# All engines in emission order: attention as a table of stages with lags, side work in slots of the weight stream, and a reordered tail

## The chip, the cores and the metric

The kernel runs on one core of one Trainium2 chip. The metric is the device time of one execution in microseconds (us). Runs of one kernel scatter by about 1% here (before: 522.9 to 529.3). Rounds ran on different chips, so kernels of different rounds are compared by their ratios to the kernel before. Each kernel has one profile, so a start or a wait is one reading. "First acc" is the start of the first weight matmul. PE is the matmul engine (PEld its weight loads), DVE the vector engine, ACT the scalar engine, POOL the GpSimd engine, SP the engine that issues the DMAs.

## The reference, cut to what matters

```python
# q, k, v: (8 batches, 8 heads, 576, 64), float32
scores = q @ k.T / 8, causal, window 128, ALiBi bias      # attention
x = softmax(scores) @ v   ->  (8, 576, 512)
X = rfft(x, axis=1)                                       # first 64 modes only
Y[m] = X[m] @ (w_r[m] + 1j * w_i[m])                      # 128 weights of 1 MB each
u = x + irfft(Y)
out = u + relu(u @ w_ch)
```

## The kernel before

It has three phases. In attention each of 16 units (a batch and four heads) is loaded, cast to bf16 (DVE), transposed (PE), evacuated from PSUM (ACT), scored (PE), exponentiated (ACT), masked (DVE), multiplied by v (PE) and normalized (DVE). Then 128 weights stream through eight buffers, while PE multiplies each with the spectra. Then a tail makes 36 output tiles. In attention every engine executes in the order in which the program emits; in the stream a scheduler places the compute instructions; the tail is in program order again.

```python
for u in range(n + 1):                     # attention, one stage a unit
    now, nxt, old = u < n, u + 1 < n, u > 0
    if u + 2 < n: at.load(u + 2)           # q, k and v of one unit together
    if now and (u % 2 == 1 or u == n - 2): load_w()
    if nxt: at.cast(u + 1, "q")                                  # DVE
    if now: at.scores(u, 0); at.scores(u, 1); at.masked(u, 0)    # PE, ACT exp, DVE mask
    if old: at.values(u - 1, 0)            # PE av, then at once DVE rec and x (the norm)
    if u > 2 and u % 2 == 1: at.spectrum((u - 3) // 2)
    if nxt: at.transpose(u + 1, "q")       # PE, then at once the ACT evacuation
    if now: at.masked(u, 1)
    if nxt: at.cast(u + 1, "k")
    if now: at.scores(u, 2)
    if nxt: at.transpose(u + 1, "k")
    if now: at.masked(u, 2); at.scores(u, 3)
    if old: at.values(u - 1, 1)
    if now: at.masked(u, 3)
    if nxt: at.cast(u + 1, "v")
# ... cut ...
for g in range(NM // 4):                   # weight stream, four modes at a time
    modes(g)                               # 32 acc matmuls, yq, transposes, YT copies
    if 8 <= g < 12: all of spectra(g - 8)
    three project(i)                       # tr, xT, mm, XW
# ... cut ...
for i in range(len(tiles)):                # tail; one PSUM tile zz for both spectra
    done = end(i)                          # inverse matmuls, relu (ACT), odd i: add x (POOL)
    begin(i + 2)
    if pending is not None: store(i - 1, *pending)    # DVE add, DMA out
    pending = done
```

The softmax here doesn't subtract the row's maximum and nothing guards it: scores larger than these inputs give would overflow.

Of the kernel before, what the change touches and what calls it, by code (L numbers as in the profile page):

```python
# [31 lines left out]
NC = 24  # L32

# [79 lines left out]
class _Attention:  # L113


    def __init__(self, tc, ctx, q, k, v, consts, x, XC):
# [11 lines left out]
        self.mask = fix.tile([P, H, 2 * P], BF16, name="mask")  # L128
# [3 lines left out]
        self.loaded, self.casted = {}, {}  # L132
# [11 lines left out]
    def masks(self, h0):  # L144

        nc = self.nc
        for h0 in (h0, h0 + 2):
            hs = slice(h0, h0 + 2)
            for n, (sign, base) in enumerate(((1, 0), (-1, -1))):
                nc.gpsimd.affine_select(  # L150
                    out=self.mask[:, hs, n * P : n * P + P],
                    in_=self.ek[:, hs, n : n + 1].broadcast_to([P, 2, P]),
                    compare_op=ALU.is_ge, fill=0.0, base=base,
                    pattern=[[0, 2], [sign, P]], channel_multiplier=-sign,
                )

    def load(self, u):
        nc = self.nc
        b, g = self.units[u]
        hs = slice(4 * g, 4 * g + 4)  # L160
        qr = self.raw.tile([P, 2, TPP, D], FP32, tag="qr")
        kr = self.raw.tile([P, 2, TPP, D], FP32, tag="kr")
        vr = self.raw.tile([P, FULL + 1, 4, D], FP32, tag="vr")
        for dst, src in ((qr, self.q), (kr, self.k)):
            nc.sync.dma_start(
                out=dst.rearrange("p e j d -> p e (j d)"),
                in_=src[b, hs].rearrange("(e h) (p j) d -> (h p) e (j d)", h=2, j=TPP),
            )
        sv = self.v[b, hs]
        for st in range(FULL + 1):  # L170
            n = P if st < FULL else TAIL
            nc.sync.dma_start(  # L172
                out=vr[:n, st],
                in_=sv[:, st * P : st * P + n].rearrange("h p d -> p h d"),
            )
        self.loaded[u] = qr, kr, vr

    def cast(self, u, w):

        nc = self.nc  # L180
        if w == "v":
            vr, vb = self.loaded.pop(u)[2], self.vb[u % 3]
            nc.vector.tensor_copy(vb[:, :FULL, :, :D], vr[:, :FULL])
            nc.vector.tensor_copy(vb[:TAIL, FULL, :, :D], vr[:TAIL, FULL])
            return
        dst = self.mid.tile([P, TPP, 2, D], BF16, tag=w, name=w)
        nc.vector.tensor_copy(dst.rearrange("p j e d -> p e j d"), self.loaded[u]["qk".index(w)])  # L187
        self.casted[u, w] = dst

    def transpose(self, u, w):  # L190
# [3 lines left out]
        for j in range(TPP):  # L194
            nc.tensor.transpose(tp[:, j], src[:, j].rearrange("p e d -> p (e d)"), self.ident)  # L195
        dst = self.qkT[u % 2][:, "qk".index(w), :, : self.S]
        nc.scalar.copy(  # L197
# [4 lines left out]
    def scores(self, u, kt):  # L202
        nc = self.nc
        b, g = self.units[u]
        qkT = self.qkT[u % 2]
        att = self.att[u % 2][:, kt * 8 * P : (kt + 1) * 8 * P]
        sc = self.ps.tile([P, 2, 512], FP32, tag="sc", bufs=2)
        for h in range(2):
# [11 lines left out]
        nc.scalar.activation(  # L220
            att, sc.rearrange("p e n -> p (e n)"), AF.Exp, scale=1.0 / math.sqrt(D)
        )

    def masked(self, u, kt):
# [4 lines left out]
        mask = self.mask[:, 4 * g : 4 * g + 4]  # L229
# [6 lines left out]
    def values(self, u, e):  # L236
# [7 lines left out]
        for h in range(2):  # L244
# [6 lines left out]
            for qt in range(FULL + 1):  # L251
# [8 lines left out]
                for n, (lhsT, kt) in enumerate(terms):  # L260
# [3 lines left out]
                    )  # L264
        cs = slice((4 * g + 2 * e) * D, (4 * g + 2 * e + 2) * D)
# [8 lines left out]
        )  # L274

    def spectrum(self, b):

        nc = self.nc
        NM = self.F.shape[2] // 2
        xt = self.ps.tile([P, 4, 2, NM], FP32, tag="tp")  # L280
        for a in range(4):
            for st in range(FULL + 1):
# [5 lines left out]
                )  # L288
        view = self.XC[:, : 4 * NC * NM].rearrange("p (a c m) -> p a c m", a=4, c=NC)
        nc.scalar.copy(view[:, :, 8 + b : 24 : 8, :], xt)  # L290
        nc.scalar.mul(view[:, :, b, :], xt[:, :, 1, :], -1.0)
        if b % 2:

            nc.vector.tensor_copy(self.x[:64, b, FULL], self.x[:64, b - 1, FULL])
# [3 lines left out]
def kernel(  # L298
# [11 lines left out]
    ctx.enter_context(tc.manual_schedule(engines={SP}))  # L310
# [13 lines left out]
    ordered = ExitStack()  # L324
    ordered.enter_context(tc.manual_schedule(engines=ALL))
    with tc.tile_pool(name="setup", bufs=1) as pool:
# [4 lines left out]
        nc.vector.tensor_copy(kv, kv_i)  # L331
        for h in range(H):
            slope = 2.0 ** (-8.0 * (h + 1) / H)
            nc.scalar.activation(ek[:, h], kv, AF.Exp, scale=slope)
        _forward_table(nc, pool, F, S)
# [16 lines left out]
    with ExitStack() as actx:  # L352
        at = _Attention(tc, actx, q, k, v, (ident, F, ek), x, XC)
        n = len(at.units)
        at.load(0)
        at.load(1)
# [4 lines left out]
        for w in "qk":  # L361
            at.cast(0, w)
            at.transpose(0, w)
        at.cast(0, "v")
        for u in range(n + 1):
            now, nxt, old = u < n, u + 1 < n, u > 0
            if u + 2 < n:
                at.load(u + 2)
            if now and (u % 2 == 1 or u == n - 2):
                load_w()  # L370
            if nxt:
                at.cast(u + 1, "q")
            if now:
                at.scores(u, 0)
                at.scores(u, 1)
                at.masked(u, 0)
            if old:
                at.values(u - 1, 0)
            if u > 2 and u % 2 == 1:
                at.spectrum((u - 3) // 2)  # L380
            if nxt:
                at.transpose(u + 1, "q")
            if now:
                at.masked(u, 1)
            if nxt:
                at.cast(u + 1, "k")
            if now:
                at.scores(u, 2)
            if nxt:
                at.transpose(u + 1, "k")  # L390
            if now:
                at.masked(u, 2)
                at.scores(u, 3)
            if old:
                at.values(u - 1, 1)
            if now:
                at.masked(u, 3)
            if nxt:
                at.cast(u + 1, "v")
            if u == 12:  # L400
                nc.gpsimd.tensor_copy(wch, wq[0])
        at.spectrum(B - 1)
        ordered.close()

    with ExitStack() as mctx:
# [13 lines left out]
        def modes(g):  # L419

            acc = ps.tile([P, DM], FP32, tag="acc")
            for j in range(4):
                m = 4 * g + j
                for ri in range(2):
                    w = wq[1 + 2 * m + ri]
                    for a in range(4):
                        c0 = (a * NC + (8 if ri == 0 else 0)) * NM + m
                        nc.tensor.matmul(  # L428
                            acc[32 * j : 32 * j + 32],
                            lhsT=XC[:, c0 : c0 + 31 * NM + 1 : NM],  # L430
                            rhs=w[:, a].bitcast(BF16)[:, 1::2],
                            start=(ri == 0 and a == 0), stop=(ri == 1 and a == 3),
                            tile_position=(0, 32 * j),
                        )
                    load_w()
            yq = pool.tile([P, DM], BF16, tag="yq")
            nc.vector.tensor_copy(yq, acc)  # L437
            tr = ps.tile([P, 4, P], BF16, tag="tr", bufs=1)
# [3 lines left out]
            for ri, copy in enumerate((nc.vector.tensor_copy, nc.scalar.copy)):  # L442
                src = tr.rearrange("p e (j c) -> p e j c", c=32)[:, :, :, ri * B : ri * B + B]
                dst = YT[:, hf, :, :, ri, mm : mm + 4]
                if hf == 1:
                    copy(dst.rearrange("p e b j -> p e j b"), src)  # L446
                else:
                    for par in range(2):
                        copy(dst[:, :, 1 - par :: 2].rearrange("p e b j -> p e j b"),  # L449
                             src[:, :, :, par::2])  # L450

        def spectra(ps, hf, bp):

            zz = ps.tile([P, 2, DM], FP32, tag="zz", bufs=1, name="zz")
            lhsT = [YT[:, hf, et, 2 * bp : 2 * bp + 2].rearrange("p b r m -> p (b r m)")
                    for et in range(4)]
            for et in range(4):
                nc.tensor.matmul(zz[:, 0], lhsT=lhsT[et], rhs=wch[:, et],  # L458
                                 start=(et == 0), stop=(et == 3))
            for et in range(4):  # L460
                nc.tensor.matmul(zz[:, 1, et * P : (et + 1) * P], lhsT=lhsT[et], rhs=ident,
                                 start=True, stop=True)
            yield
            for i in range(2):
                row = slice(64 * i, 64 * i + 64)
                b = 2 * bp + (i if hf else 1 - i)
                nc.scalar.copy(Zs[row, b, 0], zz[row, 0])  # L467
                nc.vector.tensor_copy(Zs[row, b, 1], zz[row, 1])  # L468
                yield
# [8 lines left out]
        def project(i):  # L478

            xi = tiles[i][0]  # L480
            tr = ps.tile([P, 4, P], BF16, tag="tr", bufs=1)
# [4 lines left out]
            mm = ps.tile([P, DM], FP32, tag="my", bufs=3)  # L486
# [5 lines left out]
        todo = 0  # L492
        for g in range(NM // 4):
            modes(g)
            if 8 <= g < 12:
                for _ in spectra(ps, 0, g - 8):
                    pass
            for i in range(todo, min(todo + 3, len(tiles))):
                project(i)
                todo = i + 1  # L500
# [5 lines left out]
        mctx.enter_context(tc.manual_schedule(engines=ALL))  # L506
# [5 lines left out]
        def begin(i):  # L512
            if i >= len(tiles):
                return
            mm = ps.tile([P, DM], FP32, tag="mm", name="mm")
            yy = ps.tile([P, DM], FP32, tag="yy", name="yy")
            nc.tensor.matmul(mm, lhsT=ident, rhs=XW[:, i], start=True, stop=False)
            if not pool_adds(i):
                nc.tensor.matmul(yy, lhsT=ident, rhs=tiles[i][0], start=True, stop=False)
            open_tiles[i] = mm, yy  # L520
# [11 lines left out]
        def end(i):  # L532
            xi, bs, st = tiles[i]
            mm, yy = open_tiles.pop(i)
# [19 lines left out]
        begin(0)  # L554
# [44 lines left out]
```

## Time and profile before

| | from (us) | to | length | what it is |
|---|---|---|---|---|
| attention | 0 | 159.7 | 159.7 | up to the first weight matmul |
| weight stream | 159.7 | 466.65 | 306.95 | up to the start of the last four weight matmuls |
| tail | 466.65 | 526.4 | 59.75 | 36 tiles and what precedes them |

The table by windows of the kernel before, over these phases. Columns: the stretch, its length, busy time and instructions of each engine, the granted PE clock (1 is full), the DMA share, GB/s.

```profile
core 0: us, PE busy (x) PEld busy (x) DVE busy (x) ACT busy (x) POOL busy (x), PEclk, DMA share, GB/s
0.00:159.70 159.70, 103.78 (x1345) 73.97 (x1345) 116.92 (x237) 107.73 (x124) 13.21 (x40) 0.80 0.80 238
159.70:466.65 306.95, 206.34 (x875) 89.54 (x889) 46.01 (x88) 39.04 (x69) 0.00 (x0) 0.78 0.99 410
466.65:526.40 59.75, 41.75 (x170) 16.27 (x173) 30.41 (x46) 26.16 (x45) 20.78 (x18) 0.87 0.46 159
```

Over the whole of attention and of the tail nothing is full; in the stream the DMA engines are (share 0.99, 410 GB/s). In the middle of attention, the stretch used for comparison below, the fullest compute engine, DVE, works 63.12 of 85 us (74%), and the DMA share is 0.85.

```profile
25.00:110.00 85.00, 59.85 (x776) 42.98 (x777) 63.12 (x122) 59.50 (x66) 1.89 (x1) 0.75 0.85 254
```

Waits of the kernel before (who waited for whom, total us, times, longest):

```profile
PEld L195 <- DVE k L187: 24.1, 14, 2.9
...
ACT qkT_131 L197 <- PE tp L195: 19.6, 15, 2.1
DVE rec L268 <- PE av L261: 19.6, 12, 2.3
...
DVE o L546 <- POOL r L540: 13.2, 16, 1.8
```

The page's slices of the kernel before (40 equal parts of 13.16 us):

```profile
PEclk9979567877877778868769879889779566657999
...
GB/s 260 273 287 250 263 224 259 237 250 298 282 1 235 425 425 419 419 425 420 420 422 420 421 423 421 421 355 420 424 420 421 422 422 421 423 129 87 217 208 211
```

The GB/s row shows an idle slice between attention and stream (1 GB/s: all eight weight buffers are full, and the next weight's load waits 27.1 us for PE to free one), one dip in the stream (355), and the tail at about half rate.

### The profile page before, as it was taken

The page shows a single profiled execution, that of the slowest core. Times are in us where ns is not written, and L with a number is a line of the kernel's source. Part 1 is how long each engine was busy: PE and PEld are TensorE (multiplying, and loading weights), DVE is VectorE, ACT ScalarE, POOL GpSimd, SP SyncE. Part 2 cuts the span into 40 slices and gives each one's busy share as a digit, 9 for nine tenths or more (in the row PEclk, how much of TensorE's full clock was granted, in tenths as well). Part 3 has the DMA queues.
Part 4 walks back from the last instruction along what each step waited for, and adds up shares of the span by engine and source line. Part 5 has one row for each costly group of instructions (what it writes and reads, how often), then busy time and mean ns, then how long its engine had stood idle before and what let it go on. Part 6 is the DMA issues. An engine that isn't in the chain of part 4 may idle for free.

```text
span 526.4 us, 6272 instructions
## 1 busy us (share of the span) xinstructions
PE 351.9 (67%) x2389; PEld 179.8 (34%) x2406; DVE 193.3 (37%) x370; ACT 172.9 (33%) x238; POOL 34.0 (6%) x58
## 2 busy tenths in 40 slices
PE   2675876776666864765765767676656766778773
PEld 1444654554443322322322333232323222223331
DVE  6568686878775021011011022320210110115664
ACT  5867666777732110110101112210100000005553
POOL 7010000000000000000000000000000000002443
PEclk9979567877877778868769879889779566657999
DMA  9998978799806999999999999999999999932656
GB/s 260 273 287 250 263 224 259 237 250 298 282 1 235 425 425 419 419 425 420 420 422 420 421 423 421 421 355 420 424 420 421 422 422 421 423 129 87 217 208 211
DMA packets 71087, 173.44 MB, mean 329 GB/s; under 512 B 41360, under 2 KB 41360, under 8 KB 54672
## 3 DMA queue, kind: packets, MB, share of 16 engines
q1 hardware_dynamic: 71056, 173.03, 87.1%
q8 instruction: 19, 0.31, 0.3%
q14 instruction: 12, 0.10, 0.1%
HBM read 163.58 MB, written 9.44 MB: 329 GB/s over the span
## 4 chain that ended last, share of the span: by engine, by line
DMA 47%; PE 25%; DVE 11%; ACT 7%; issue 5%; SPq 3%; POOL 2%; POOLq 0%; DVEq 0%; ACTq 0%
DMA w<-in_moe_w_i_dram 46%; PE acc L428 6%; PE av L261 4%; PE tp L195 3%; PE sc L215 2%; SPq L172 2%; PE zz L458 2%; ACT att_133 L220 2%; PE xt L283 2%; POOL r L540 2%; DVE att_133 L231 1%; DVE Zs L468 1%; PE mm L488 1%; ACT Zs L467 1%; DVE x L269 1%
## 5 line engine op out<-in xcount | busy, mean ns | idle before, releaser
L428 PE MATMUL acc<-w,XC 128*32 128x512 bf16 x512 | 140.8, 453 | 56.5 <-DMA w<-in_moe_w_i_dram 32.5
L428 PEld LDWEIGHTS <-XC 128*32 128x32 bf16 x512 | 55.6, 141 | 125.2 <-issue 106.5
L437 DVE CAST yq<-acc 128x512 bf16<-128x512 f32 x16 | 11.1, 692 | 164.1 <-PE acc L428 164.0
L488 PE MATMUL mm<-wch,xT 128*128 128x512 bf16 x133 | 44.9, 465 | 9.1 <-DVE xT L485 8.4
L490 ACT CAST XW<-mm 128x512 bf16<-128x512 f32 x36 | 21.1, 585 | 78.1 <-PE mm L488 78.1
L540 POOL TENSOR_TENSOR r<-r,x 128x512 f32<-128x512 f32 x18 | 20.8, 1154 | 342.9 <-ACT r L537 341.6
L485 DVE COPY xT<-tr 128x512 bf16<-128x512 bf16 x36 | 15.3, 425 | 71.8 <-PE tr L483 71.8
L446 ACT COPY YT<-tr 128x128 bf16<-128x128 bf16 x8 | 5.8, 727 | 100.6 <-DVE YT L446 100.6
L220 ACT ACTIVATE att_132<-sc 128x1024 bf16<-128x1024 f32 x32 | 32.1, 1033 | 0.3
L220 ACT ACTIVATE att_133<-sc 128x1024 bf16<-128x1024 f32 x32 | 31.9, 1029 | 0.5
L449 ACT COPY YT<-tr 128x64 bf16<-128x64 bf16 x16 | 5.8, 530 | 79.1 <-DVE YT L449 79.1
L483 PE MATMUL tr<-ident,x 128*128 128x128 bf16 x144 | 18.7, 271 | 19.0 <-ACT YT L449 12.7
L195 PE MATMUL tp<-ident,k 128*128 128x128 bf16 x144 | 15.8, 282 | 22.4 <-DVE k L187 9.0
L546 DVE TENSOR_TENSOR o<-yy,r 128x512 f32<-128x512 f32 x36 | 23.6, 687 | 13.5 <-POOL r L540 13.2
L537 ACT ACTIVATE r<-mm 128x512 f32<-128x512 f32 x36 | 21.5, 597 | 19.5 <-PE mm L527 18.2
L269 DVE TENSOR_TENSOR x<-av,rec 128x640 bf16<-128x640 f32 x32 | 26.4, 825 | 1.1
L195 PE MATMUL tp<-ident,q 128*128 128x128 bf16 x144 | 12.7, 243 | 21.0 <-DVE q L187 15.2
L231 DVE TENSOR_TENSOR att_133<-att_133,mask 128x1024 bf16<-128x1024 bf16 (+2 forms) x40 | 22.4, 578 | 10.2 <-ACT att_133 L220 9.9
L231 DVE TENSOR_TENSOR att_132<-att_132,mask 128x1024 bf16<-128x1024 bf16 (+2 forms) x40 | 23.2, 598 | 6.9 <-ACT att_132 L220 6.7
L483 PEld LDWEIGHTS <-x 128*128 128x128 bf16 x144 | 14.7, 123 | 30.4 <-issue 19.1
L488 PEld LDWEIGHTS <-xT 128*128 128x128 bf16 x144 | 13.1, 111 | 34.0 <-DVE xT L485 20.0
L197 ACT COPY qkT_131<-tp 128x1152 bf16<-128x1152 bf16 x16 | 17.9, 1119 | 19.6 <-PE tp L195 19.6
(95 smaller groups left out, 388.3 us busy)
## 6 DMA issues: line engine op xcount, KB each, us to landing
w<-in_moe_w_r_dram SPq DMA_DIRECT2D x64, 1024.0 KB, 15.2
w<-in_moe_w_i_dram SPq DMA_DIRECT2D x64, 1024.0 KB, 16.6
qr<-in_q_dram SPq DMA_DIRECT2D x16, 576.0 KB, 5.0
kr<-in_k_dram SPq DMA_DIRECT2D x16, 576.0 KB, 6.2
vr<-in_v_dram SPq DMA_DIRECT2D x64, 128.0 KB, 4.0
out_dram<-o SPq DMA_DIRECT2D x32, 256.0 KB, 2.1
vr<-in_v_dram SPq DMA_DIRECT2D x16, 64.0 KB, 3.8
w<-in_moe_w_ch_dram SPq DMA_DIRECT2D x1, 1024.0 KB, 6.0
```

Of the source, the lines that this page charges most:

```text
L195: nc.tensor.transpose(tp[:, j], src[:, j].rearrange("p e d -> p (e d)"), self.ident)
L220: nc.scalar.activation(att, sc.rearrange("p e n -> p (e n)"), AF.Exp, scale=1.0 / math.sqrt(D))
L231: nc.vector.tensor_tensor(out=heads[:, :, c0 : c0 + n], in0=heads[:, :, c0 : c0 + n], in1=mask[:, :, m0 : m0 + n], op=ALU.mult,)
L261: nc.tensor.matmul(dst, lhsT=lhsT, rhs=vb[:, kt, hv, : D + 1], start=(n == 0), stop=(n == len(terms) - 1),)
L269: nc.vector.tensor_tensor(out=self.x[:, b, :, cs].rearrange("p t (h d) -> p h t d", h=2), in0=tiles[:, :, :, :D], in1=rec.unsqueeze(-1).br ...
L428: nc.tensor.matmul(acc[32 * j : 32 * j + 32], lhsT=XC[:, c0 : c0 + 31 * NM + 1 : NM], rhs=w[:, a].bitcast(BF16)[:, 1::2], start=(ri == 0 a ...
L483: nc.tensor.transpose(tr[:, dt], xi[:, dt * P : (dt + 1) * P], ident)
L488: nc.tensor.matmul(mm, lhsT=xT[:, dt], rhs=wch[:, dt], start=(dt == 0), stop=(dt == 3))
L490: nc.scalar.copy(XW[:, i], mm)
L537: nc.scalar.activation(r, mm, AF.Relu)
L540: nc.gpsimd.tensor_tensor(out=r, in0=r, in1=xi, op=ALU.add)
L546: nc.vector.tensor_tensor(out=o, in0=yy, in1=r, op=ALU.add)
```

## The change

Its intent: let no engine wait right behind another. Every compute method is split into its PE part and its DVE or ACT part (transpose and evacuate, score and exp, value and norm, spectrum and channels). A table gives the order in a stage, with a lag in units for each entry: 1 is the unit before, -3 the unit three ahead. In the stream, side work is cut into pieces and one piece goes into the slot behind each weight; where none is left, near the end, "warm" matmuls keep PE busy. In the tail the spectra get two PSUM tiles instead of one, yy gets four buffers and mm two (three each before), and a tile with a POOL add is stored one iteration later. (The field of masks is renamed `table`, cut here.)

```diff
+STAGE = (
+    ("mask", 3, 1), ("exp", 1, 0), ("score", 0, 0), ("exp", 0, 0), ("spectrum", None, 2),
+    ("value", 0, 1), ("cast", "v", 0), ("score", 2, 0), ("channels", None, 2),
+    ("transpose", "k", -1), ("cast", "k", -2), ("mask", 1, 0), ("exp", 2, 0), ("norm", 0, 1),
+    ("cast", "q", -3), ("score", 3, 0), ("evacuate", "k", -1), ("mask", 0, 0), ("value", 1, 1),
+    ("exp", 3, 0), ("transpose", "q", -2), ("evacuate", "q", -2), ("mask", 2, 0),
+    ("score", 1, -1), ("norm", 1, 1),
+)
 # each cast is now followed at once by the load of the same input two units on:
+        self.load(w, u + 2)
-        for u in range(n + 1):
-            # ... cut: the order shown above ...
+        for w in "qkv":
+            for u in range(2):
+                at.load(w, u)
+        for stage in range(min(lags), n + max(lags)):
+            for name, arg, lag in STAGE:
+                u = stage - lag
+                if 0 <= u < n:
+                    getattr(at, name)(u, arg)
+            if stage > 0 and (stage % 2 == 1 or stage == n - 2):
+                load_w()
 # stream, behind the four matmuls of each weight:
+                if quads:
+                    if next(quads[0], True): quads.pop(0)
+                elif side:
+                    if next(side[0], True): side.pop(0)
+                elif 8 * g + i >= 2 * NM - 5:
+                    if 8 * g + i < 2 * NM - 1: warm()      # 6 matmuls, result unused
 # YT copies: all on DVE, with the modes j innermost
-                    copy(dst.rearrange("p e b j -> p e j b"), src)
+                    nc.vector.tensor_copy(dst, src)        # src is "p e c j"
 # tail
-            begin(i + 2)
-            if pending is not None:
-                store(i - 1, *pending)
+                begin(i + 1, "mm")          # 2 buffers
+                begin(i + 2, "yy")          # 4 buffers
+            for k in (i - 1, i - 2):
+                if k in pending and (k == i - 2 or not pool_adds(k)):
+                    store(k, *pending.pop(k))
```

## The prediction

> **What bounds the kernel now.** Three phases in series (table by windows, timeline). (1) Attention, to 159.7 us, where the first weight matmul (acc) begins. From 25 to 150 us no engine is full: DVE 68 to 82% busy, ACT 68 to 77%, PE 65 to 76%, DMA share 0.64 to 0.97. A stage repeats every 8.55 us (two from 104.1 to 121.2 us). The waits: PE transposes wait for DVE casts of the same stage, ACT evacuations for those transposes, DVE rec for PE av (17.8 us): latencies chained across in-order engines. (2) Weight stream, to 466.7 us: DMA share 1.00 at 415 to 425 GB/s, 46% of the span in the chain of waits. One dip (355 GB/s, 342 to 355 us), where spectra and projections held up PE. DMA idles from 144 to 161 us, all eight buffers full. (3) Tail, to 526.4 us: yq, tr, YT, zz, Zs in series until the first inverse matmul at 474.9 us, then 36 tiles at about 1.3 us each. DVE needs 0.69 us a tile, ACT 0.60; DVE o waits for POOL r (13.2 us), PE yy for DVE o (8.3 us). PE's clock is 0.50 from 465 to 481 us.
>
> **What the change does.** It removes nearly no work, adds up to 24 warm matmuls and moves order.
>
> *Attention.* Casts run 2 to 3 stages ahead, transposes 1 to 2, so no stage waits for its own casts. Start to start I read per stage 6.6 us of DVE (casts 2.15, masks 2.5, norms 2.0) and 6.5 us of ACT (four exps of 0.97, two evacuations of 1.05, half of XC). Loads limit too: 1.77 MB at the observed 297 GB/s plus half a weight, 7.2 us. With handoffs I estimate 7.5 us a stage. Casting further ahead costs at the start (q of unit 2 waits for 4.1 MB), so stage 0 ends no earlier. First weight matmul at 144 us, 15.5 us earlier; the idle DMA gap before it remains.
>
> *Stream.* 120 loads at 2.49 us is 298 us, the floor. Slots between weights remove the dip: 307 becomes 303 us, 4 us.
>
> *Tail.* Per two tiles PE has 7 matmuls of 0.216 us, DVE 1.4 us, POOL 1.16 us; with the pool tile's store delayed and four yy buffers I expect 0.95 us a tile. Separate z and zw let ACT and DVE copy at once. [...] the warm matmuls should save 2 to 3 us. YT copies on DVE cost nothing: they were serialized already. 59.7 becomes 48 us, 11.5 us.
>
> The phases are in series, so all is on the critical path: 15.5 + 4 + 11.5 = 31.
>
> **Prediction:** 495 us, 8 in 10 between 484 and 510. Faster by over 2%: 0.91; within 2%: 0.07; slower: 0.02.
>
> **What would show it.** First acc near 144 us (140 to 151); stage period 7.2 to 7.9 us, PE's waits for casts gone; stream about 303 us at 420 GB/s without a dip; clock near 1.0 at the last weights and in the tail; tail 45 to 51 us, DVE about 75% busy in it.
>
> **What would make it wrong.** Attention still bound by latency, or by loads (256-byte v packets), at over 8 us a stage; a DVE queue blocked on a late load at the start; PE stalling in order behind the inverse table on DVE; warm matmuls delaying the last quad; the tail still chained through ACT and POOL.

The ground for the 2 to 3 us of the warm matmuls was not shown by a run, so those 2 to 3 us stand as the author's estimate. What the trace of the kernel before does show is a clock of 0.50 from 465 to 481 us, PE being busy 5.87 of the last 6.00 us of that, and then 1.00 from 481 to 485 us. The 2 to 3 us are not a term of their own in the sum: they lie within the tail's 11.5, and 15.5 + 4 + 11.5 came to 31.

## More of the kernel before

What fills a stage when no engine is full is in the chain of waits of the kernel before (start, length, what; each piece was released by the one before). It is one stage, from a cast of q to the next, 8.95 us (the one after it takes 8.14):

```profile
104.12 0.68 DVE q L187
...
104.85 0.69 PE tp L195 x9
...
105.66 0.97 issue
106.63 1.04 ACT att_132 L220
...
107.71 1.14 PE tp L195 x9
108.85 0.54 PE sc L215 x8
109.39 1.12 PE av L261 x18
...
110.53 0.23 DVE rec L268
...
111.52 0.75 DVE att_132 L231 x2
112.27 0.61 DVE vb_129 L183
...
113.07 0.67 DVE q L187
```

Read it as a loop: the cast of q (DVE) releases its transposes (PE), then ACT's evacuation and exp, the transposes of k (PE), values (PE), norm, mask and cast of v (DVE), and behind those, only because DVE works in order, stands the next cast of q. (In this trace DVE ran a stage's instructions in the emitted order, from the cast of q at 104.04 us to the next at 112.99, and stood idle for 2.14 us before the norm at 110.53, with a mask, the cast of v and that cast of q behind it.)

## The result

489.0 us median (487.15 to 491.28, 4 runs) against 525.5 (522.94 to 529.3, 4 runs). The ratio is 0.9302, 95% interval 0.9224 to 0.938. (A ratio here is the mean time of one kernel's fast runs over that of the other's in the same rounds, so not quite the ratio of the medians quoted.)

The table by windows of the changed kernel, over its three phases and over the comparison stretch:

```profile
core 0: us, PE busy (x) PEld busy (x) DVE busy (x) ACT busy (x) POOL busy (x), PEclk, DMA share, GB/s
0.00:136.97 136.97, 88.73 (x1345) 67.53 (x1345) 116.55 (x239) 103.13 (x122) 12.72 (x40) 0.90 0.95 277
136.97:441.68 304.71, 216.19 (x896) 93.07 (x913) 42.74 (x110) 28.14 (x46) 0.00 (x0) 0.90 1.00 413
441.68:485.50 43.82, 34.92 (x172) 14.91 (x174) 30.14 (x47) 25.15 (x44) 20.82 (x18) 0.98 0.63 217
25.00:110.00 85.00, 59.00 (x950) 45.20 (x949) 77.34 (x151) 70.88 (x79) 1.96 (x1) 0.89 1.04 295
```

DVE's work in attention is the same 117 us; it is done in 137 us in place of 160. In the profiled runs attention lost 22.7 us, the stream 2.2, the tail 15.9: 40.9 together, of which the medians keep 36.5 (the profiled run before took 528.08 us, 2.6 above its median; the changed one 487.15, 1.9 below). All profiles show how firm this is: the old stream took 307.0 to 309.5 us in three, the new one 304.1 to 307.3 in eleven, so the stream's 2.2 us are near the scatter; the tail took 58.2 to 59.8 us in the same three, and 43.5 to 44.2 in the nine that have the changed tail whole.

The chain of waits of the changed kernel, a piece of attention. It runs along DVE itself, instruction behind instruction, broken only by loads of k:

```profile
85.84 4.88 DMA kr<-in_k_dram
...
90.75 0.76 DVE k L200
91.51 0.60 DVE att_130 L252
...
92.27 0.82 DVE x L296
93.10 0.67 DVE q L200
93.77 1.20 DVE att_130 L252 x2
```

The waits of the changed kernel that answer to those shown. PE now waits for DVE's norm, but with DVE full that costs little, and DVE hardly waits for PE. The new waits are of DVE for loads:

```profile
PE av L282 <- DVE x L296: 23.7, 18, 3.8
...
DVE k L200 <- DMA kr<-in_k_dram: 6.5, 5, 2.3
...
DVE q L200 <- DMA qr<-in_q_dram: 5.0, 1, 5.0
...
DVE o L569 <- ACT r L560: 4.3, 13, 0.8
...
DVE rec L295 <- PE av L282: 2.8, 3, 1.3
```

The page's slices of the changed kernel (12.14 us each). The dip in the stream is gone, the idle gap before it is not; the clock row is near full in attention and at the end:

```profile
PEclk9997987998869989989989999988888978769999
...
GB/s 252 315 285 269 320 286 327 291 288 259 234 171 423 421 421 420 422 422 420 421 422 422 421 423 421 421 421 421 422 419 423 423 421 420 422 422 98 241 277 263
```

### The profile page after: what moved, and what is told of

It reads as the page before. It is cut to its first block, busy times and chain, and to the rows that moved or that the text cites. A ratio compares the mean times of both kernels' runs of the same rounds, so it can differ in the third digit from the quotient of the medians.

```text
span 485.5 us, 6274 instructions
## 1 busy us (share of the span) xinstructions
PE 339.8 (70%) x2411; PEld 175.5 (36%) x2430; DVE 189.4 (39%) x395; ACT 156.4 (32%) x212; POOL 33.5 (7%) x58
## 4 chain that ended last, share of the span: by engine, by line
DMA 58%; PE 16%; DVE 14%; ACT 4%; issue 4%; SPq 3%; POOL 1%; POOLq 0%; DVEq 0%; ACTq 0%
DMA w<-in_moe_w_i_dram 45%; DMA w<-in_moe_w_r_dram 8%; PE acc L496 6%; DMA kr<-in_k_dram 4%; DVE x L296 3%; DVE att_130 L252 3%; DVE att_131 L252 2%; SPq L178 2%; DVE k L200 2%; DVE q L200 1%; PE av L282 1%; DMA qr<-in_q_dram 1%; PE warm L486 1%; PE mm L540 1%; PE mm L550 1%
## 5 line engine op out<-in xcount | busy, mean ns | idle before, releaser
L496 PE MATMUL acc<-w,XC 128*32 128x512 bf16 x512 | 153.3, 433 | 85.8 <-DMA w<-in_moe_w_r_dram 42.2
L496 PEld LDWEIGHTS <-XC 128*32 128x32 bf16 x512 | 64.7, 137 | 151.8 <-issue 125.8
L481 ACT CAST XW<-my 128x512 bf16<-128x512 f32 x36 | 21.1, 585 | 237.3 <-PE my L479 208.8
L479 PE MATMUL my<-wch,xT 128*128 128x512 bf16 x129 | 38.6, 405 | 2.9 <-DVE xT L475 1.5
L282 PEld LDWEIGHTS <-att_131 128*128 128x128 bf16 x288 | 12.9, 109 | 27.9 <-DVE x L296 25.5
L458 ACT CAST Zs<-zw 64x512 bf16<-64x512 f32 x16 | 9.2, 577 | 40.3 <-PE zw L449 40.1
L215 ACT COPY qkT_128<-tp 128x1152 bf16<-128x1152 bf16 x15 | 16.8, 1117 | 15.9 <-PE tp L209 15.8
L209 PE MATMUL tp<-ident,q 128*128 128x128 bf16 x144 | 14.0, 259 | 11.1 <-DVE q L200 7.8
L459 DVE CAST Zs<-z 64x512 bf16<-64x512 f32 x16 | 11.0, 687 | 22.5 <-PE z L452 22.3
L215 ACT COPY qkT_129<-tp 128x1152 bf16<-128x1152 bf16 x16 | 18.2, 1135 | 1.6 <-PE tp L209 1.6
L315 PE MATMUL xt<-F,x 128*128 128x128 bf16 x160 | 12.7, 246 | 4.7 <-DVE x L296 3.4
```

Source lines behind the costliest of these rows:

```text
L215: (self.nc.vector.tensor_copy if (u, w) == (0, "q") else self.nc.scalar.copy)(dst.rearrange("q h (p j) -> q h p j", j=TPP), tp.rearrange(" ...
L282: nc.tensor.matmul(dst, lhsT=lhsT, rhs=vb[:, kt, hv, : D + 1], start=(n == 0), stop=(n == len(terms) - 1),)
L479: nc.tensor.matmul(mm, lhsT=xT[:, dt], rhs=wch[:, dt], start=(dt == 0), stop=(dt == 3))
L481: nc.scalar.copy(XW[:, i], mm)
L496: nc.tensor.matmul(acc[32 * (i // 2) : 32 * (i // 2) + 32], lhsT=XC[:, c0 : c0 + 31 * NM + 1 : NM], rhs=w[:, a].bitcast(BF16)[:, 1::2], st ...
```

## The experiments

Twelve kernels ran, each correct. The table gives the profile's start of the first weight matmul ("first acc", the end of attention), DVE's busy share from 25 to 110 us, and times.

| run | first acc, us | DVE 25 to 110 | median, us | ratio to before (95%) |
|---|---|---|---|---|
| before | 159.7 | 74% | 525.5 | |
| changed | 137.0 | 91% | 489.0 | 0.9302 (0.9224 to 0.9380) |
| attn_only | 136.9 | 90% | 506.43 | 0.9649 (0.9588 to 0.9709) |
| nolead | 139.5 | 91% | 490.65 | 0.9356 (0.9313 to 0.9399) |
| nolead1 | 140.6 | 90% | 492.54 | 0.9383 (0.9337 to 0.9429) |
| before_filler | 156.0 | 80% | 523.55 | 0.9961 (0.9905 to 1.0017) |
| old_order | 160.5 | 74% | 508.47 | 0.9630 (0.9572 to 0.9687) |
| old_norms | 179.6 | 66% | 531.96 | 1.0080 (1.0027 to 1.0134) |
| old_lead | 143.2 | 86% | 495.46 | 0.9386 (0.9336 to 0.9436) |
| old_both | 179.9 | 65% | 530.77 | 1.0063 (1.0015 to 1.0111) |
| old_slip | 143.3 | 84% | 497.92 | 0.9493 (0.9428 to 0.9558) |
| no_warm | 140.2 | 89% | 491.55 | 0.9368 (0.9327 to 0.9409) |
| old_store | 139.2 | 87% | 491.31 | 0.9342 (0.9285 to 0.9398) |
| late_start | 131.3 | 97% | 484.65 | 0.9225 (0.9183 to 0.9267) |

Four of these have the very attention order of the change (changed, attn_only, no_warm, old_store): 136.9 to 140.2. So differences of first acc below some 3 us say nothing.

### attn_only: one part alone

```diff
# the kernel before, with the changed attention phase; its stream and tail as before
-    ctx.enter_context(tc.manual_schedule(engines=ALL | {SP}))
+    ctx.enter_context(tc.manual_schedule(engines={SP}))    # ALL for attention only
```

> The kernel before with the new attention order alone; its weight stream and tail stay as they were, placed by the scheduler. If the three phases simply add, the first weight matmul comes at about 137 us as in the changed kernel (159.7 before), the stream keeps its 307 us and the tail its 60 us, and the whole is 22 to 23 us (4.3%) faster than before: about 503 us. If the earlier attention end were given back later, or the other parts needed it, the gain would be under 15 us.

Measured: first acc 136.9, so attention's gain is there whole without the rest, and 506.43 us in all, half of the change's gain. By the medians that is 17.8 us, short of the 22 to 23 expected. The old stream then took about 309 us, some 2 more than before, and the tail kept its length. The parts add: attention alone gives 3.5%, the rest without the new order (old_order, below) 3.7%, all together 7.0%.

### nolead: is it the casts' lead?

My prediction rested on the casts' lead ("so no stage waits for its own casts").

```diff
-    ("transpose", "k", -1), ("cast", "k", -2), ("mask", 1, 0), ...
-    ("cast", "q", -3), ("score", 3, 0), ...
-    ("exp", 3, 0), ("transpose", "q", -2), ...
+    ("cast", "k", -1), ("transpose", "k", -1), ("mask", 1, 0), ...
+    ("score", 3, 0), ...
+    ("exp", 3, 0), ("cast", "q", -2), ("transpose", "q", -2), ...
```

> The changed kernel, with the casts of k and q moved back into the stage of their own transposes, directly ahead of them; all else the same. Theory (lead): the transposes wait for DVE casts again, DVE loses its full load, the middle stage period rises from 7.4 us to about 8.2 us, the first weight matmul comes 8 to 14 us later than 137 us, the whole near 499 us. Rival (the order of the other stages and the smaller number of waits does it, the casts' lead does nothing): the same within 3 us, or faster by the 3 to 5 us that the late loads at the start cost.

Measured: 139.5, within the scatter. The lead of the casts is not needed. The theory, as I had put it, fell. The waits of PE and its weight loads for casts of k and q did come back, 38.0 us listed from 16 to 125 us (41.3 before, none listed in the changed kernel), and cost next to nothing. (The two rows can wait at the same time, as at 31.86 us in the kernel before, where both had waited for one cast of q, 1.08 and 0.96 us. So such sums compare kernels; they are not time lost.)

### before_filler: is it the clock?

```diff
# the kernel before
-        tp = self.ps.tile([P, TPP, P], BF16, tag="tp")
+        tp = self.ps.tile([P, 16, P], BF16, tag="tp")
+        for _ in range(8):
+            nc.tensor.matmul(<unused part of tp>, lhsT=self.ident, rhs=self.ident)
```

> The kernel before with eight extra 128-column matmuls of the identity ahead of each group of nine transposes, into an unused part of the same PSUM tile, in PE's idle time there; order unchanged. The granted clock in attention was 0.65 to 0.86 before and 0.86 to 0.93 after. Rival (clock): if the faster PE is what shortened attention, the clock rises to about 0.9 and the first weight matmul comes at about 145 us or earlier. Theory (order): even with the clock raised it comes no earlier than 154 us, since the waits for DVE and ACT stay; if the clock does not rise the run tells nothing.

The comparison stretch of before_filler (columns as above):

```profile
25.00:110.00 85.00, 59.09 (x988) 45.12 (x985) 68.04 (x131) 62.83 (x68) 2.25 (x1) 0.98 0.90 270
```

The clock rose from 0.75 to 0.98, above the changed kernel's 0.89, and first acc came 3.7 us earlier, not 22.7. That alone doesn't rule the clock out, because the fillers were not all in idle time: 11.4 us of them lie in the chain of waits of attention, so the clock could be worth up to some 15 us (an estimate, 3.7 + 11.4). The kernel before settles more. Five of its stages between 23 and 140 us had a granted clock of 1.00, and they took 8.15 to 8.94 us from norm to norm, 8.35 in the mean (four of them without a spectrum, which is the lighter kind of stage for PE). Two of them, and under them one of the changed kernel:

```profile
97.13:105.31 8.18, 4.80 (x83) 3.42 (x82) 6.98 (x15) 6.43 (x8) 0.00 (x0) 1.00 0.84 252
114.26:122.41 8.15, 4.77 (x83) 3.50 (x82) 6.80 (x15) 6.39 (x8) 0.00 (x0) 1.00 0.95 288
92.03:98.69 6.66, 4.34 (x85) 3.70 (x86) 6.59 (x14) 6.11 (x8) 0.00 (x0) 1.00 1.12 327
```

The mean of the first 12 stages, at any clock, fell from 9.00 to 7.44 us. By this count the full clock alone leaves some 0.9 of these 1.56 us to the order; a faster PE can have a part in the gain, but isn't the cause of most of it.

### no_warm

```diff
-                elif 8 * g + i >= 2 * NM - 5:
-                    if 8 * g + i < 2 * NM - 1:
-                        warm()
```

> The changed kernel without the 24 warm matmuls. Expected: the clock at the last weights stays at 0.5 to 0.6, the tail's first 8 to 12 us run at half clock, the first inverse matmul comes 6 to 8 us after the last weight group's start in place of 4.6, and the whole is 2.5 to 4 us slower. If the tail is bound by DVE and ACT alone, the difference is under 1 us.

The table by windows of no_warm: its last weights, then the stretch up to its first inverse matmul:

```profile
430.00:445.50 15.50, 10.85 (x27) 3.24 (x24) 0.00 (x0) 0.00 (x0) 0.00 (x0) 0.61 0.83 346
445.50:449.60 4.10, 2.71 (x15) 1.01 (x15) 1.54 (x4) 0.58 (x1) 0.00 (x0) 0.93 0.00 0
```

The last weights ran at 0.61 (in the last 3.5 us the weight loads of one weight started 0.38 to 0.43 us apart, as they did in the kernel before at a clock of 0.50), but in this run the clock was near full right after them all the same; it did not stay low into the tail as expected. The first inverse matmul came 5.3 us after the last weights' start (444.3 to 449.6) in place of 4.6, and the whole tail took 46.3 us in place of 43.8. The 2.5 us look like the prediction's 2 to 3, but only 0.7 of them lie ahead of the first inverse matmul. From the first to the last store the clock was 1.00 in the changed kernel; in no_warm it was 1.00 from 449.6 to 465 us and 0.92 in the mean of what follows (0.96 in the changed kernel, from 465 us to its end). Between the stores of no_warm DVE waited once, at 481.7 us, for an earlier output to leave its buffer:

```profile
DVE o L566 <- DMA out_dram<-o: 1.9, 1, 1.9
```

(In the changed kernel that wait is 0.5 us.) So the traces show about 0.7 us for the warm matmuls; that the sum came near the prediction is luck. The median is 2.5 us higher than the changed kernel's of another round, but the intervals of the ratios overlap.

### old_order, old_norms, old_lead, old_both: the old order in the new program

The changed program can run the old order: it is only another table. That makes a control and three single moves.

```diff
# old_order, as (stage, argument, lag)
+ cast q -1, score 0 0, exp 0 0, score 1 0, exp 1 0, mask 0 0, value 0 1, norm 0 1,
+ spectrum 2, channels 2, transpose q -1, evacuate q -1, mask 1 0, cast k -1, score 2 0,
+ exp 2 0, transpose k -1, evacuate k -1, mask 2 0, score 3 0, exp 3 0, value 1 1,
+ norm 1 1, mask 3 0, cast v -1
# old_norms: norm 0 moved behind cast k, norm 1 behind cast v
# old_lead:  cast q -2 and cast k -2, in the same places
# old_both:  both
```

> The changed kernel with the attention stages put back in the order of the kernel before (casts in the stage ahead of their use, norm right behind its value, exp right behind its score), but with the new load order, weight stream and tail: a control. If the order alone explains attention, the first weight matmul is back at 157 to 162 us (137 changed, 159.7 before), and the whole is 18 to 23 us slower than the changed kernel, about 508 us. If it is the loads (issued one by one behind their casts) that matter, it stays under 150 us.

Measured: 160.5, and 508.47 us in all, as expected. So it is the order that gained; loading each input right behind a cast, which this run kept, gained nothing under the old order.

> As old_order, with one thing moved: each norm is put on DVE behind the next cast in place of right behind its value, so DVE has other work while PE computes. New theory (after the run that took the lead away lost only 2.5 us): DVE is the fullest engine and what counts is that it never waits right behind another engine. Before, DVE rec waited 17.8 us for PE av. Then the first weight matmul comes 8 to 14 us earlier than in old_order. Rival (the casts' lead is the cure): under 4 us.

Measured: 179.6, 19 us worse. The sign was wrong. Waits of old_norms from 25 to 110 us:

```profile
DVE att L271 <- ACT att L259: 28.0, 15, 3.6
...
ACT qkT L234 <- PE tp L228: 17.0, 15, 3.0
PE av L301 <- DVE x L315: 16.0, 8, 2.2
```

There is one PSUM buffer for av. With norm 1 behind mask 3 and the cast of v, the next value on PE waits for the buffer (16.0 us in 8 waits); PE works in order, so the transposes behind it wait; so do ACT's evacuations (17.0 us) and exps, and so do the masks on DVE (28.0 us). DVE's wait for PE av is no longer on the list, and a longer loop had been closed: in the timeline of old_norms, norm 1 at 80.99 us releases PE's values (82.11) and, behind them, its spectrum (83.09), then come ACT (85.39), PE's transposes (86.31 and 88.24), ACT's exps, masks and the cast of v (91.93), and at 92.73, 11.74 us later, the next norm 1.

> As old_order, with only the casts of q and k moved one stage ahead of their transposes. If the lead is the cure, PE's waits for DVE casts vanish (47 us of listed waits of PE and its weight loads before) and the first weight matmul comes 10 us or more earlier than in old_order. New theory: the waits of DVE for PE av and for ACT exp stay, so 2 to 6 us.

Measured: 143.2, 17.3 us earlier than the control's 160.5. So the lead is enough by itself, though nolead shows that it isn't needed.

> As old_order, with both: norms moved and casts a stage ahead. New theory: DVE reaches over 88% busy between 25 and 110 us and the first weight matmul is within 4 us of the changed kernel's 137 us; the rest of the computed order adds little. If the order of exps, masks and scores matters by itself, over 145 us.

Measured: 179.9; the late norms decide, and the lead doesn't help them.

### nolead1: no lead at all

nolead had left q transposed one stage ahead of its scores. Here nothing is ahead:

```diff
-    ("exp", 3, 0), ("cast", "q", -2), ("transpose", "q", -2), ("evacuate", "q", -2), ...
+    ("exp", 3, 0), ("cast", "q", -1), ("transpose", "q", -1), ("evacuate", "q", -1), ...
```

> The computed order with no lead at all: the run without cast lead still transposed q one stage ahead of its scores, so its lead had only moved; here q's cast, transposes and evacuation all come at the end of the stage ahead, as near to the scores as in the old order. Theory (what counts is slack in the loop cast, transpose, evacuate, score, exp, wherever in it the slack sits): ACT waits for transposes again, the stage grows by 1 us or more, and the first weight matmul comes at 147 to 156 us (139.5 with q one stage ahead, 137.0 changed, 160.5 old order). If the lead is not what matters, it stays under 143 us.

Measured: 140.6, a miss: still at the edge of the scatter. The waits return, but in small pieces (ACT waited 7.8 us for scores from 16 to 125 us) that don't add up to a lost stage. Distance in stages is not the measure.

### old_slip: cut the loop with a small move

What old_order has, and the others, as I read the tables, don't, is the loop of the chain of waits above: each cast stands on DVE *behind* an instruction that waits for PE or ACT work which itself waits for that cast's predecessor. If so, moving each cast past a few DVE instructions must do nearly all that a stage of lead does. (Here each cast of q and k passes three entries of the table.)

```diff
# old_order
+ cast k -1        (head of the stage; was behind mask 1)
- cast q -1        (head of the stage)
  ... mask 2 0
+ cast q -2        (behind mask 2, ahead of norm 1, mask 3, cast v)
```

> As old_order, with two casts moved on DVE by a few instructions only: cast k from behind mask 1 to the head of the stage (ahead of mask 0, norm 0, mask 1), and cast q from the head of a stage to behind mask 2 of the stage ahead (ahead of norm 1, mask 3, cast v). Theory (a loop round three in-order engines, once a stage): DVE's casts stand behind DVE instructions that wait for PE or ACT, PE's transposes wait for the casts, and the PE and ACT work that those DVE instructions wait for stands behind the transposes; the chain of waits of the old order goes from one cast of q to the next in 8.96 us so. A slip of three instructions cuts it: DVE over 83% busy from 25 to 110 us (74% in old_order) and the first weight matmul at 142 to 150 us (160.5 in old_order, 143.2 with casts a whole stage ahead). Rival (a whole stage of lead, or the computed order's other moves, are needed): 155 us or later.

Measured: 143.3, against 143.2 with a whole stage of lead. The comparison stretch, first of old_order, then of old_slip:

```profile
25.00:110.00 85.00, 60.92 (x771) 43.61 (x772) 63.31 (x122) 59.36 (x65) 3.11 (x1) 0.73 0.84 247
```

```profile
25.00:110.00 85.00, 62.12 (x905) 44.77 (x901) 71.02 (x142) 67.62 (x75) 1.89 (x1) 0.90 1.01 283
```

DVE goes from 63.3 to 71.0 us busy of 85, and the listed waits of PE and its weight loads for casts of k and q fall from 36.3 us in old_order to 2.0 (from 16 to 125 us). The clock went up too, 0.73 to 0.90, and may have its part in this (see before_filler). So cutting the loop is the shown cause of a large part of attention's gain, but how large is less sure than the 17.2 us of the two profiles say. Old_order's profiled run was the slowest of its four (513.25), old_slip's the fastest (494.85). By the ratios old_slip gets back 42% of what old_order lost (0.9630 to 0.9493, of 0.9630 to 0.9302), old_lead 74%; by DVE's busy time it is 55%. Which of the computed order's other moves cut it in nolead1 (mask 3 deferred, score 1 ahead, the places of the norms) was not separated, nor what makes the last 3 to 6 us between 143 and 137 to 140.

### old_store: the tail's stores

```diff
-            for k in (i - 1, i - 2):
-                if k in pending and (k == i - 2 or not pool_adds(k)):
-                    store(k, *pending.pop(k))
+            if i - 1 in pending:
+                store(i - 1, *pending.pop(i - 1))
```

> The changed kernel with the tail's stores in the old order (tile i-1 always, also where POOL adds), its four yy and two mm buffers kept. Theory: DVE waits for POOL r again (13 us before, 0.6 after), a tile takes about 1.2 us in place of 0.96, the whole is 6 to 10 us slower. Rival (the four yy buffers, or the full clock, made the tail faster): under 2 us slower.

Waits of old_store in its tail:

```profile
DVE o L569 <- POOL r L563: 7.9, 13, 1.4
```

The wait for POOL returned, but from the first to the last store it took 35.9 us (1.03 us a tile), against 33.5 (0.96) in the changed kernel and 45.1 (1.29) before. So the delayed stores are worth about 2.4 of those 11.6 us (33.35 to 33.95 in the nine profiles with the whole changed tail), and the 6 to 10 us expected of them were a miss. The rest comes from what this run kept: four yy buffers, two mm buffers begun apart, two PSUM tiles for the spectra, the full clock from the first tile. Those were not separated.

### late_start: a version that beats both

The chain of the changed kernel is DVE's own work, plus waits for loads of k and q. Nine weight loads compete with those, though DMA is idle later on. So the loads alone were moved.

```diff
+LATE = {9: 1, 10: 1, 11: 1, 12: 2, 13: 2, 14: 2}        # stage: weight loads
-            if stage > 0 and (stage % 2 == 1 or stage == n - 2):
-                load_w()
+            if stage == -2:
+                at.load("v", 1)
+            for _ in range(LATE.get(stage, 0)):
+                load_w()
-        for w in "qkv":
-            for u in range(2):
-                at.load(w, u)
+        for w, u in (("q", 0), ("k", 0), ("q", 1), ("k", 1), ("v", 0)):
+            at.load(w, u)
```

> The changed kernel with nothing but loads reordered: the nine weight loads of the attention phase moved from stages 1 to 15 to stages 9 to 14, so they do not compete with k and q; and at the start k of unit 0 loaded ahead of q of unit 1, and v of unit 1 behind q of unit 2. Theory (the middle stages of the changed kernel are bound by DVE's 6.6 us, plus stalls on loads): DVE's 5.4 us of waits for k loads and 2 to 4 of the 5.0 us wait for q at the start go, the mean middle stage falls from 7.4 to under 6.9 us, and the first weight matmul comes at about 129 us (125 to 132) in place of 137. The stream and the tail keep their lengths, so the whole is 6 to 9 us faster, about 481 us. If the loads as a whole limit the phase, it stays at 134 to 138 us.

The comparison stretch of late_start:

```profile
25.00:110.00 85.00, 57.13 (x1030) 43.31 (x1030) 82.77 (x164) 77.71 (x88) 2.28 (x1) 0.99 1.03 284
```

DVE is busy 97%: the first ten stages from norm to norm took 6.58 to 6.91 us, the floor of about 6.6 us as expected. Then two took 8.3: in one, two masks on DVE took 2.98 us beside a POOL cast (see the last section), in the other DVE waited for k and v (1.2 us). The mean of twelve was 6.92, where under 6.9 was expected. First acc came at 131.3 us, 5.7 earlier than in the changed kernel's profile and outside the scatter of its order. New, smaller waits for the last loads of v (3.3 us in all) are the price of weights now loaded beside them. The whole is 484.65 us (481.39 to 485.73, 6 runs), 4.35 us less than the changed kernel's median, short of the 6 to 9 expected. The two intervals of ratios (0.9183 to 0.9267; 0.9224 to 0.938) come from different rounds and overlap; that it is faster than the changed kernel rests on the times, which don't overlap, and on the profile. The gain is 0.9%.

## Why the prediction was right or wrong

- **The whole: right, and too small.** 495 us was predicted, 489.0 measured, inside the range; 31 us of gain became 36.5. The parts were further off than the sum: attention and the tail gained more than predicted, the stream less.
- **Attention: 15.5 us predicted, 22.7 in the profile.** The middle stage was right: 7.5 us predicted, and from unit 0's first norm (25.13 us) to unit 12's (114.44) 12 stages took 89.3 us, 7.44 each. That this is so near is in part luck. The estimate was DVE's 6.6 us and handoffs between the engines; in these 12 stages DVE was idle 7.7 us, 5.4 of them in waits for loads of k, and 1.7 us more went into masks beside a POOL cast. The mis-sized term is the end. I took 7.5 us for all 16 stages, but casts that ran ahead have run out in the last three: those took 5.6, 5.4 and 4.8 us from norm to norm. DVE's own sum without the casts of q and k is 6.6 - 2 x 0.67 = 5.3 us. Three stages of 7.5 are 22.5 us, measured 15.8: 6.7 of the missing 7.2 us.
- **Its mechanism: half right.** "So no stage waits for its own casts" was the given reason. Lead alone does give 17.3 us (old_lead), but it isn't needed (nolead, nolead1). What has to go is the loop round the in-order engines, and a slip past three entries of the table brings first acc as early (old_slip, with the reserve made there). PE's waits for casts going away was a symptom: in nolead they are back (38.0 us listed), and first acc is not later than the scatter.
- **Loads as a second limit: right in kind.** DMA share was 1.04 in the middle; DVE waits for k and q appeared (5.4 us from 16 to 125 us, and 5.0), and late_start took most of them away (1.0 and 2.4 are left).
- **Stream: 4 us predicted, 2.2 in the profile;** 303 us became 304.7. The dip went as predicted; the 2.2 us are near the scatter of the stream (see the result). PE stood behind the inverse table on DVE for only about 1.5 us there, and the stream's slices stay at 419 to 423 GB/s.
- **Tail: 11.5 us predicted, 15.9 in the profile.** The rate was right (0.95 us a tile predicted, 0.96 measured). The rest is entry and drain, for which 48 us left about 14 (48 less 36 tiles of 0.95): all but the 33.5 us of the stores took 10.3. From the last weights' start to the first inverse matmul it took 4.6 us in place of 8.2. The first copies out of the separate z and zw did run at once (ACT from 445.64, DVE from 445.86 us), where those out of zz took turns (ACT at 474.24, DVE at 474.85, ACT at 475.57 us). "YT copies on DVE cost nothing" was wrong to the good side: as the loop order changed, too, the copy on DVE got from 0.73 to about 0.29 us. The last quad, before and after:

```profile
469.95 0.73 DVE L446 COPY YT<-tr 128x128 bf16<-128x128 bf16 x1 [0.70 <-PE tr L440]
...
470.71 0.73 ACT L446 COPY YT<-tr 128x128 bf16<-128x128 bf16 x1 [19.12 <-DVE YT L446]
```

```profile
444.02 0.49 DVE L437 COPY YT<-tr 128x128 bf16<-128x128 bf16 x2 [0.49 <-PE tr L431]
```

  (Twice 0.73 us in series, against 0.49 for both.) Of the predicted 2 to 3 us of the warm matmuls, no_warm shows 0.7.
- **The clock.** That dense matmuls soon bring the full clock was the estimate, and the traces don't bear it out as a rule. They show 0.50 in long stretches, then 1.00: before, PE was at 0.50 from 465 to 475 us and at 0.51 from 475 to 481, although it was busy 5.87 of those last 6.00 us, and at 1.00 from 481 to 485. In the changed kernel, whose warm matmuls began at 432.9 us, the clock was 0.78 from 430 to 436 us and 1.00 from there to the last weights (441.7). In no_warm it was 0.93 over 4 us that followed a sparse stretch at 0.61 (PE busy 10.85 of 15.50 us). So "dense matmuls, hence full clock at once" is a bet, not a rule.

## What to carry to other kernels

When no engine is full, follow the chain of waits from one instance of an instruction to its next: if it returns to the same engine once a stage, that is a loop round in-order queues, and its length is the stage (8.95 us before). Cut it by moving the instruction that feeds the other engines ahead of those that wait for them; three places sufficed here (old_slip: 143.3 us for first acc in place of 160.5), and look at single-buffered PSUM tiles before moving a consumer later, as that can close a longer loop (11.74 us in old_norms). When the chain then runs along one engine, its sum of work is the floor (DVE's 6.6 us; late_start's stages took 6.58 us at the least), and what is left is to keep loads that aren't urgent out of the way of those that are.

## What else the traces measured

- In the changed kernel two masks on DVE took 2.98 us in place of 1.28 while POOL cast w_ch for 1.96 us, right on the critical engine (2.98 in late_start too; in the kernel before, one mask took 1.48 us in place of 0.68 beside the same cast).

```profile
39.94 2.98 DVE L252 TENSOR_TENSOR att_131<-att_131,mask 128x1024 bf16<-128x1024 bf16 x2
...
40.41 1.96 POOL L408 CAST wch<-w 128x2048 bf16<-128x2048 f32 x1 [26.82 <-DMA w<-in_moe_w_ch_dram]
```

- Here the gaps of the fullest engine pointed at DVE's wait for PE av. My remedy, to move the norms later, cost 19 us (old_norms). What that view lacks is the loop, which the chain over a whole stage shows (8.95 us before).
- The clock rose after unlike stretches: before, it stayed at 0.51 through 6 us that were 98% busy (475 to 481 us) and was 1.00 only behind them; in no_warm it was 0.93 right after 3.5 us in which PE was busy about 2.9 (442.0 to 445.5 us).
- A bf16 copy out of PSUM on DVE depended on the loop order: 128x128 took 0.73 us with the modes outside (mean of 8, before) and about 0.29 us (mean of 16) with the four modes innermost.
